# Loads behind the table, limits over three engines, late full stores and a staggered first unit in an attention and feed-forward kernel

## The chip, the core and the metric

One Trainium2 chip, of which the kernel uses one core. The metric is the time of one execution in device microseconds (us). Five engines run their own instruction streams and meet at semaphores: TensorE (PE; its weight loads are listed as PEld), VectorE (DVE), ScalarE (ACT), GpSimd (POOL) and SyncE (SP), which here only issues DMAs.

## The reference

Attention with a learned relative bias for 4 batches, 8 heads, 576 positions and head size 64, then a feed-forward part with a cosine gate over the 2304 rows.

```
scores = q @ k.T / sqrt(64)
x      = log1p(|i-j|) / log1p(max(i,1))         # per row i and column j
bias   = relu(x * w1 + b1) @ w2                 # 32 hidden values -> 8 heads
scores = scores + bias                          # the same for all batches
attn   = softmax(scores);  out = attn @ v       # [4, 8, 576, 64]
x      = out as [2304, 512]
h      = x @ w_in                               # 512 -> 2048
result = (h * cos(h)) @ w_out                   # 2048 -> 512
```

All in float32. The kernel gets two small tables besides: `ltab` = log1p of 0..575, and `pack` with 1/log1p(max(i,1)), w1, b1 and w2 laid out by partition.

## The kernel before

There are three stages: the bias rows, the attention units, the feed-forward part.

**Bias rows (to about 51 us).** The bias depends on the positions and the head alone. Since relu(x*w1+b1) scales, the kernel takes `wl = ltab*w1` (one value per hidden unit and distance) and `edge` = log1p(i)*b1 and computes for each query i a hidden row `ht = max(wl + edge[i], 0)`. Sixteen queries make a group: four `ht` tiles of 128 partitions (four queries of 32 hidden units each), three or four of them on VectorE (line 341) and the rest on ScalarE (line 339); TensorE multiplies by the negated w2 (line 356); ScalarE scales with `mrow` and writes `rt` (line 374), and SP stores the 128 rows of 591 values to a scratch tensor `sc` in DRAM (line 375). There are 36 groups, in the order of bias tiles 4, 0, 1, 2, 3. A bias tile `bt` (128 queries x 576 keys of one head) is then read back from `sc` with a skewed pattern (`load_bias`, lines 273 and 286). Line 397 says after which group which bias tile is loaded.

At the start ScalarE's queue issues the load of `lt` (`ltab` to all partitions), SP that of `pk` (`pack`), and both go on with k and q of the first two units. VectorE prepares `edge` in four quarters of 32 partitions and a corner (lines 326 and 327), ScalarE `wl` (line 328).

**Units (51 to about 290 us).** A unit is a pair of heads hp and a batch b, 16 in all, hp outermost; each has five tiles of queries in the order 0, 1, 4, 2, 3. One (unit, tile) is a job and gets a slot; `slot(i)` (line 616) writes the order of the work by hand: the scores of job i (`qk`, line 431), exp of job i-1 on ScalarE (line 471), its scaling by 1/sum on GpSimd (line 494), the turning of job i-3's probabilities on TensorE (`halves`, line 501) with copies to SBUF on ScalarE and VectorE, the product with v (line 569), and the split of q and k of later units in high and low parts on GpSimd (lines 186, 190). `qk` writes two score tiles `s`, one per head, of which there are two buffers in all; each head takes six matmuls with 64 rows (two halves of the keys, three products of high and low parts), and the heads alternate. VectorE adds the bias and takes the row minimum of the negated scores (line 453) and with that frees the buffer.

`load_w` brings a weight in float32, `abs_w` (line 92, ScalarE) is the first to read it, in slot 9, and line 100 (VectorE) goes on. Line 724 issues the first two weights in slots 5 and 6.

**Feed-forward (to the end).** Matmuls with w_in (line 759) and w_out (line 805) take turns on TensorE.

All DMAs but those of ScalarE's queue are issued by SP in program order. Eight semaphores are used in turn for the DMAs, so that an issue waits until the DMA eight before it has landed.

Of the kernel before, what the change touches and what calls it, by code (L numbers as in the profile page):

```python
# [9 lines left out]
F32 = mybir.dt.float32  # L10
# [3 lines left out]
AF = mybir.ActivationFunctionType  # L14
ALU = mybir.AluOpType
# [13 lines left out]
def kernel(  # L29
# [11 lines left out]
    nc = tc.nc  # L41
    B, H, S, D = q.shape
# [4 lines left out]
    NQ = S // 16  # L47
    RB = S + 15
    PITCH = S + 32
    GP = 16 * (8 * PITCH - 1)  # L50
    HALF = S // 2
# [14 lines left out]
    xT = const.tile([128, HP, NT], F32, name="xT")  # L66
    xs = const.tile([128, 2, KD, TB], F32R, name="xs")
    wpre = [const.tile([128, 2, 2, 512], F32R, name=f"wpre{i}") for i in range(WPRE)]
    sc = [dram.tile([1, (8 if t < 4 else 4) * GP + 16], F32, name=f"sc{t}") for t in range(5)]
# [7 lines left out]
    def load_w(fc, part):  # L77
        r = wk.tile([128, 512, 2], U32, tag="raw", name="raw")
        if part == 0:
            nc.sync.dma_start(  # L80
                out=r.rearrange("p (c x) y -> p c (x y)", c=KD),
                in_=w_in[:, fc * 256 : fc * 256 + 256].rearrange("(c p) x -> p c x", p=128),
            )
        else:
            nc.sync.dma_start(out=r.rearrange("p x y -> p (x y)"), in_=w_out[fc * 128 : fc * 128 + 128, :])
        raw[fc, part] = r
# [25 lines left out]
    with tc.manual_schedule():  # L112
# [14 lines left out]
        lt = ca.tile([128, S], F32, name="lt")  # L127
# [5 lines left out]
        qTs = [st.tile([128, 2, 640], F32R, name=f"qT{i}") for i in range(2)]  # L133
# [19 lines left out]
        def load(u, x, pieces=None, queue=None):  # L153
            hp, b = units[u]
            src = {"q": q, "k": k, "v": v}[x]
            pair_ = src[b, 2 * hp : 2 * hp + 2]
            if x == "v":
                t = vN[u % 2]
                for h in range(2):
                    nc.sync.dma_start(  # L160
                        out=t[:, 4 * h : 4 * h + 4, :], in_=pair_[h, 0:512].rearrange("(c p) d -> p c d", p=128)
                    )
                for h in range(2):
                    nc.sync.dma_start(out=t[64 * h : 64 * h + 64, 8 + h, :], in_=pair_[h, 512:576])
                return
            if (u, x) not in nat:
                m = 5 if x == "k" else 4
                nat[u, x] = (lk if x == "k" else ld).tile([128, m, 2, D], F32, tag=x, name=f"n{x}")
            t = nat[u, x]
            todo_ = [(t[:, 0:4, h], pair_[h, 0:512].rearrange("(p r) d -> p r d", r=4)) for h in range(2)]  # L170
            if x == "k":
                for i, o in ((q, 0), (k, 64)):
                    todo_.append((t[o : o + 64, 4], i[b, 2 * hp : 2 * hp + 2, 512:576].rearrange("h p d -> p h d")))
            for o, i in todo_ if pieces is None else [todo_[n] for n in pieces]:
                (queue or nc.sync).dma_start(out=o, in_=i)
# [16 lines left out]
        kN = {}  # L192
# [104 lines left out]
        ra = opened(stage, "ra", 8, "left")  # L297
# [3 lines left out]
        wl = ca.tile([128, S], F32, name="wl")  # L301
        pk = ca.tile([128, pack.shape[1]], F32, name="pk")
        edge = ca.tile([128, S // 4], F32, name="edge")
        nbd = ca.tile([128, 32], F32, name="nbd")
        nc.sync.dma_start(out=pk[:, 0:178], in_=pack[:, 0:178])
        load(0, "k")
        load(0, "q", queue=nc.scalar)
        for x in "kq":
            load(1, x)
        wparts = [(fc, p) for fc in range(WPRE) for p in range(2)]  # L310
        mi, w1c, b1c = pk[:, 0:144], pk[:, 144:145], pk[:, 145:146]
        bd = pk[:, 146:178]
# [7 lines left out]
        for s in range(4):  # L320
            nc.tensor.matmul(
                pm[32 * s : 32 * s + 32, 0:NQ], pick, mi[:, s : 4 * NQ : 4], start=True, stop=True, tile_position=(0, 32 * s)
            )
        for g in range(4):
            r = slice(32 * g, 32 * g + 32)
            nc.vector.tensor_scalar(edge[r], lt[r, g:S:4], b1c[r], None, ALU.mult)
        nc.vector.tensor_scalar(edge[0:32, 0:1], lt[0:32, 1:2], b1c[0:32], None, ALU.mult)
        nc.scalar.activation(out=wl, in_=lt, func=AF.Copy, scale=w1c)

        def bias_hid(k):  # L330
            qi = groups[todo[k][0]][todo[k][1]]
# [13 lines left out]
        def bias_rows(k, hts):  # L345
# [17 lines left out]
                    )  # L363
            return ps[:, at : at + RB]

        def bias_store(k, ps):
            t, gi = todo[k]
            qi = groups[t][gi]
            rt = ra.tile([128, RB], F32, tag="r", name="rt")
            m = mrow[:, qi : qi + 1]  # L370
            if k == len(todo) - 2:
                nc.vector.tensor_scalar(rt, ps, m, None, ALU.mult)
            else:
                nc.scalar.activation(out=rt, in_=ps, func=AF.Copy, scale=m)
            nc.sync.dma_start(
                out=bass.AP(sc[t].tensor, sc[t].offset + gi * GP, [[PITCH, 128], [1, RB]]),
                in_=rt,
            )

        tiles = [0, 1, 4, 2, 3]  # L380
        for i in range(WPRE):
# [4 lines left out]
        SECOND = {6: ("k", (0,)), 7: ("k", (1,)), 8: ("k", (2,)), 9: ("k", (3,)), 10: ("q", (0,)), 11: ("q", (1,))}  # L386
        todo = [(t, gi) for t in (4, 0, 1, 2, 3) for gi in range(len(groups[t]))]
        held, hts = None, bias_hid(0)
        nc.vector.tensor_copy(mrow, pm[:, 0:NQ])
        for n in range(len(todo) + 1):  # L390
            now = hts
            if n < len(todo):
                hts = bias_hid(n + 1) if n + 1 < len(todo) else None
                ps = bias_rows(n, now)
            if held:
                bias_store(*held)
            for t, heads in {13: ((4, ()),), 20: ((0, (0,)),), 21: ((0, (1,)),), 28: ((1, (0,)),), 29: ((1, (1,)),)}.get(n, ()):
                load_bias(0, t, heads)
            if n == len(todo):
                load_bias(0, 2)  # L400
                load(3, "k", (2, 3))
                load_bias(0, 3)
            held = (n, ps)
            if n in SECOND:
                load(2, *SECOND[n])
            if n in T_FIRST:
                halved[n] = turn(*T_FIRST[n], bank())
                keep_hi(*T_FIRST[n], halved[n])
            if n - 1 in T_FIRST:
                keep_lo(*T_FIRST[n - 1], halved[n - 1])  # L410
# [16 lines left out]
            PX[u, hf] = px.tile([128, WQ[hf]], F32, tag=f"x{hf}", name=f"PX{hf}")  # L427

        cur = {}

        def qk(u, j):
            t = tiles[j]
            heads = range(2 if t < 4 else 1)
            s = [ps_s.tile([128, 2, 512], F32, tag="s", name="s") for h in heads]
            for hf in range(2):
                for n, (a, b) in enumerate(((0, 0), (0, 1), (1, 0))):
                    for h in heads:
                        r = slice(64 * h, 64 * h + 64) if t < 4 else slice(0, 128)
                        o = HALF * hf + (64 if h == 0 else 0)
                        nc.tensor.matmul(  # L440
                            s[h][:, hf, 0:HALF],
                            qTs[u % 2][r, a, 128 * t : 128 * t + 128] if t < 4 else qTs[u % 2][:, a, 512:640],
                            kN[u][r, b, o : o + HALF],
                            start=(n == 0),
                            stop=(n == 2),
                            tile_position=(r.start, 0),
                        )
            hp = units[u][0]
            P[u, j] = pp.tile([128, 1152], F32, tag="p", name="P")
            for h in heads:  # L450
                neg = P[u, j][:, 576 * h : 576 * h + 576]
                m = sv.tile([128, 2], F32, tag=f"m{h}", name="m")
                nc.vector.tensor_tensor_reduce(  # L453
                    neg.rearrange("p (a x) -> p a x", a=2),
                    s[h][:, :, 0:HALF],
                    bias[hp, t, h].rearrange("p (a x) -> p a x", a=2),
                    1.0,
                    3.0e38,
                    ALU.add,
                    ALU.min,  # L460
                    m[:, 0:1],
                )
                cur[u, j, h] = (neg, m)
# [131 lines left out]
        W_MID = [(3, 9)]  # L595
        W_PLAN = [(0, 2), (0.5, 3), (1, 7), (2, 8), ("load", 8), (4, 12)]
        W_LATE = 10
        REST = {2: (1, 2), 3: (3, 4)}
        get = lambda i: jobs[i] if 0 <= i < len(jobs) else None

# [15 lines left out]
        def slot(i):  # L616
# [101 lines left out]
            if now:  # L718
                if i == 1:
                    load(0, "v")  # L720
                for du, x in LOAD_PLAN[j]:
                    if u + du < NU:
                        load(u + du, x, (0, 1) if (u, x) == (0, "k") else None)
                if i in (5, 6):
                    load_w(*wparts[i - 5])
                hp, b = units[u]
                if b == B - 1 and hp + 1 < HP:
                    load_bias(hp + 1, tiles[j])
                if i in X_EARLY:
                    split_x(0, 0, X_EARLY.index(i))  # L730
# [228 lines left out]
```

## Time and profile before

| | |
|---|---|
| median of 3 runs | 695.43 us (694.91 to 697.91) |
| the profiled execution | 695.13 us, its span 693.3 us |
| TensorE busy | 679.7 us (98%) |
| VectorE, ScalarE, GpSimd busy | 580.8 (84%), 435.8 (63%), 398.2 us (57%) |
| DMA | 58.57 MB, 84 GB/s on average; 345 to 351 GB/s from 30 to 50 us |
| granted clock of TensorE | 1.0 throughout |

The shares are averages over stages with different limits: in the bias rows VectorE, ScalarE and TensorE are all nearly full; in the first unit none is, and from there on TensorE is. Busy time counts no DMA issues.

### The profile page before, as it was taken

What the parts mean: (1) busy time and instruction counts of PE and PEld (TensorE: products, weight loads), DVE (VectorE), ACT (ScalarE), POOL (GpSimd) and SP (SyncE); (2) the same over time, 40 slices, a digit from 0 to 9 for tenths busy, and PEclk for the clock granted to TensorE, in tenths of its full rate; (3) what the DMA queues carried; (4) which work ended last, traced back from release to release, by engine and by line L of the source; (5) the groups of instructions that cost most, each with busy time, mean ns of one, the idle gap of its engine ahead of it and who ended that gap; (6) DMA issues with size and microseconds to landing.
All of it is one profiled execution on the core that took longest, in us unless ns stands there. A gap on an engine that the chain in (4) does not pass through costs nothing.

```text
span 693.3 us, 15601 instructions
## 1 busy us (share of the span) xinstructions
PE 679.7 (98%) x5747; PEld 561.9 (81%) x5747; DVE 580.8 (84%) x1345; ACT 435.8 (63%) x938; POOL 398.2 (57%) x480
## 2 busy tenths in 40 slices
PE   6998999999999999999999999999999999999997
PEld 3666777777777777799989898998988888999986
DVE  8998888888888888678788789999899899876666
ACT  6998888988889887545565554454544544433342
POOL 0008888898988989646456356265374474463300
PEclk9999999999999999999999999999999999999999
DMA  6798546437337311012011111110111110011112
GB/s 161 266 350 224 130 122 168 104 85 220 71 92 200 99 50 41 10 31 61 30 34 60 30 49 44 32 61 32 34 58 31 57 35 32 0 46 46 47 46 92
DMA packets 84445, 58.57 MB, mean 84 GB/s; under 512 B 62224, under 2 KB 70800, under 8 KB 84368
## 3 DMA queue, kind: packets, MB, share of 16 engines
q1 hardware_dynamic: 83024, 56.88, 28.4%
q8 instruction: 46, 0.75, 0.5%
q10 hardware_dynamic: 1344, 0.69, 0.4%
q14 instruction: 31, 0.25, 0.1%
HBM read 41.94 MB, written 15.61 MB: 83 GB/s over the span
## 4 chain that ended last, share of the span: by engine, by line
PE 93%; DMA 3%; DVE 1%; POOL 1%; ACT 1%; issue 0%; SPq 0%; DVEq 0%; POOLq 0%
PE ph L759 29%; PE po L805 29%; PE pv L569 12%; PE s L440 11%; PE pm L501 6%; PE pa L356 4%; DMA sc<-rt 2%; PE pt L501 1%; PE spare L501 1%; DMA lt<-in_ltab_dram 1%; DMA bt<-sc 1%; POOL P L494 0%; DVE ht L341 0%; ACT ht L339 0%; DVE acc L829 0%
## 5 line engine op out<-in xcount | busy, mean ns | idle before, releaser
L453 DVE CUSTOM_DVE_ANT_0 P<-s,bt 128x576 f32<-128x576 f32 x144 | 103.8, 753 | 24.4 <-PE s L440 24.1
L494 POOL TENSOR_SCALAR P<-P,rc 128x576 f32<-128x576 f32 x144 | 108.3, 764 | 24.3 <-DVE rc L487 11.5
L763 ACT ACTIVATE a<-ph,quarter 128x384 int32<-128x384 f32 x96 | 55.7, 581 | 97.8 <-PE ph L759 96.9
L555 POOL TENSOR_TENSOR xs<-xT,xs 128x384 fp32r<-128x384 f32 x96 | 108.1, 1126 | 8.0
L471 ACT ACTIVATE P<-P,m 128x576 f32<-128x576 f32 x144 | 110.0, 768 | 0.6 <-DVE m L453 0.6
L759 PE MATMUL ph<-xs,wpre 128*128 128x384 f32 x576 | 109.4, 338 | 0.0
L759 PE MATMUL ph<-xs,w 128*128 128x384 f32 x576 | 108.5, 337 | 0.0
L774 ACT ACTIVATE r<-r,hpi 128x384 f32<-128x384 f32 x96 | 59.3, 617 | 74.8 <-DVE r L770 74.6
L759 PEld LDWEIGHTS ph<-xs,wpre 128*128 128x128 f32 x576 | 101.9, 188 | 5.4 <-DVE a L778 0.9
L759 PEld LDWEIGHTS ph<-xs,w 128*128 128x128 f32 x576 | 101.3, 188 | 5.1 <-DVE a L778 1.2
L769 DVE SCALAR_TENSOR_TENSOR r<-a,ph 128x384 f32<-128x384 int32 x96 | 52.8, 550 | 62.7 <-ACT a L763 62.6
L440 PE MATMUL s<-kN,qT 64*128 64x288 f32 (+1 forms) x864 | 92.0, 311 | 2.0 <-DVE m L453 1.4
L440 PEld LDWEIGHTS s<-kN,qT 64*128 64x128 f32 (+1 forms) x864 | 70.7, 185 | 27.2 <-DVE dn L484 7.6
L554 POOL TENSOR_SCALAR xs<-xT 128x384 fp32r<-128x384 f32 x96 | 63.2, 658 | 29.7 <-PE ph L759 29.7
L788 DVE TENSOR_TENSOR gl<-a,gh 128x384 fp32r<-128x384 f32 x96 | 75.8, 789 | 0.4 <-ACT gh L782 0.4
L569 PE MATMUL pv<-PT,vN 128*64 128x320 f32 (+1 forms) x512 | 76.0, 418 | 0.0
L805 PE MATMUL po<-wpre,gh 128*128 128x512 f32 x288 | 75.3, 397 | 0.0
L805 PE MATMUL po<-w,gh 128*128 128x512 f32 x288 | 75.2, 395 | 0.0
L110 POOL TENSOR_TENSOR w<-wb,w 128x512 fp32r<-128x512 f32 x16 | 20.8, 1297 | 87.6 <-ACT w L108 87.6
L782 ACT ACTIVATE gh<-a 128x384 fp32r<-128x384 f32 x96 | 49.8, 518 | 23.6 <-DVE a L778 23.6
L770 DVE SCALAR_TENSOR_TENSOR r<-a,r 128x384 f32<-128x384 int32 x96 | 61.0, 636 | 3.3
L805 PEld LDWEIGHTS po<-wpre,gh 128*128 128x128 f32 x288 | 53.4, 188 | 9.4 <-issue 0.5
(98 smaller groups left out, 1166.8 us busy)
## 6 DMA issues: line engine op xcount, KB each, us to landing
sc<-rt SPq DMA_DIRECT2D x36, 295.5 KB, 4.5
raw<-in_moe_w_in_dram SPq DMA_DIRECT2D x16, 512.0 KB, 3.7
raw<-in_moe_w_out_dram SPq DMA_DIRECT2D x16, 512.0 KB, 3.5
bt<-sc SPq DMA_DIRECT2D x16, 288.0 KB, 4.0
out_dram<-acc SPq DMA_DIRECT2D x17, 256.0 KB, 2.0
nk<-in_k_dram SPq DMA_DIRECT2D x32, 128.0 KB, 3.5
bt<-sc SPq DMA_DIRECT2D x16, 256.0 KB, 4.2
vN<-in_v_dram SPq DMA_DIRECT2D x32, 128.0 KB, 2.8
```

The source lines that it names most:

```text
L440: nc.tensor.matmul(s[h][:, hf, 0:HALF], qTs[u % 2][r, a, 128 * t : 128 * t + 128] if t < 4 else qTs[u % 2][:, a, 512:640], kN[u][r, b, o : ...
L453: nc.vector.tensor_tensor_reduce(neg.rearrange("p (a x) -> p a x", a=2), s[h][:, :, 0:HALF], bias[hp, t, h].rearrange("p (a x) -> p a x", ...
L471: nc.scalar.activation(out=P[u, j][:, 576 * h : 576 * h + 576], in_=neg, func=AF.Exp, bias=m[:, 0:1], scale=-1.0, accum_out=dn[u, j][:, h ...
L494: nc.gpsimd.tensor_scalar(p, p, r, 1.0, ALU.mult, ALU.mult)
L554: nc.gpsimd.tensor_scalar(h, src, 1.0, 1.0, ALU.mult, ALU.mult)
L555: nc.gpsimd.tensor_tensor(l, src, f(h), ALU.subtract)
L569: nc.tensor.matmul(ps[64 * h : 64 * h + 64, 0 : WQ[hf]], a, m, start=(c == 0), stop=(c == 4), tile_position=(0, 64 * h), skip_group_check= ...
L759: nc.tensor.matmul(ps, a, x, start=(i == 0), stop=(i == 3 * KD - 1))
L770: nc.vector.scalar_tensor_tensor(r, n, -TWO_PI_LO, r, ALU.mult, ALU.add)
L774: nc.scalar.activation(out=r, in_=r, func=AF.Sin, scale=SIN_SCALE, bias=hpi)
L788: nc.vector.tensor_tensor(gl, a, f(G[key][0]), ALU.subtract)
L805: nc.tensor.matmul(O[n][i], a[:, 128 * i : 128 * i + 128], w, start=(i0 == 0 and p == 0), stop=(i0 == GF - 1 and p == 2),)
```

## The change

Three parts. (1) At the start: SP waits for `lt` before it issues any load of k or q (`keepalive_nop` with `lt` as its input), and also issues the q of the first unit, which ScalarE's queue did. `wl` is made by VectorE; the quarters of `edge` by VectorE (two), ScalarE and GpSimd; the corner of `edge` and `mrow` by ScalarE, behind its first `ht`. (2) The last eleven groups of rows are written into the not yet used part of `xT` and not into the pool `ra`. At once only the rows of the first pair of heads are stored (two DMAs of 16 rows each); the full store of all 128 rows follows in slots 6 to 14. The loads of bias tile 2 move up to groups 33 and 34, and the first two weights are issued in slots 8 and 9. (3) In the first unit the second head's six matmuls lag three behind the first head's.

```diff
         nc.sync.dma_start(out=pk[:, 0:178], in_=pack[:, 0:178])
-        load(0, "k")
-        load(0, "q", queue=nc.scalar)
-        for x in "kq":
-            load(1, x)
+        nc.sync.keepalive_nop(ins=[nc.sync.lower_ap(lt)])
+        for u in range(2):
+            for x in "kq":
+                load(u, x)
...
+        nc.vector.tensor_scalar(wl, lt, w1c, None, ALU.mult)
         for g in range(4):
             r = slice(32 * g, 32 * g + 32)
-            nc.vector.tensor_scalar(edge[r], lt[r, g:S:4], b1c[r], None, ALU.mult)
-        nc.vector.tensor_scalar(edge[0:32, 0:1], lt[0:32, 1:2], b1c[0:32], None, ALU.mult)
-        nc.scalar.activation(out=wl, in_=lt, func=AF.Copy, scale=w1c)
+            if g == 3:
+                nc.gpsimd.tensor_scalar(edge[r], lt[r, g:S:4], b1c[r], 1.0, ALU.mult, ALU.mult)
+            elif g == 2:
+                nc.scalar.activation(out=edge[r], in_=lt[r, g:S:4], func=AF.Copy, scale=b1c[r])
+            else:
+                nc.vector.tensor_scalar(edge[r], lt[r, g:S:4], b1c[r], None, ALU.mult)
...
+        rest = xT[:, 1:].rearrange("p h n -> p (h n)")
+        late = [rest[:, RB * i : RB * i + RB] for i in range(11)]
+
+        def store_rows(k, rt):
+            t, gi = todo[k]
+            nc.sync.dma_start(
+                out=bass.AP(sc[t].tensor, sc[t].offset + gi * GP, [[PITCH, 128], [1, RB]]),
+                in_=rt,
+            )
+
         def bias_store(k, ps):
             t, gi = todo[k]
             qi = groups[t][gi]
-            rt = ra.tile([128, RB], F32, tag="r", name="rt")
+            n = k - len(todo) + len(late)
+            rt = late[n] if n >= 0 else ra.tile([128, RB], F32, tag="r", name="rt")
...
+            if n < 0:
+                store_rows(k, rt)
+            else:
+                for h in range(2):
+                    nc.sync.dma_start(
+                        out=bass.AP(sc[t].tensor, sc[t].offset + gi * GP + h * PITCH, [[8 * PITCH, 16], [1, RB]]),
+                        in_=rt[h:128:8],
+                    )
...
-        nc.vector.tensor_copy(mrow, pm[:, 0:NQ])
+        nc.scalar.activation(out=edge[0:32, 0:1], in_=lt[0:32, 1:2], func=AF.Copy, scale=b1c[0:32])
+        nc.scalar.activation(out=mrow, in_=pm[:, 0:NQ], func=AF.Copy)
...
+        STAGGERED = (0,)
...
+            lag = 3 if u in STAGGERED and t < 4 else 0
+            for x in range(6 + lag):
+                for h in heads:
+                    if not 0 <= x - lag * h < 6:
+                        continue
+                    hf, n = divmod(x - lag * h, 3)
...
+        STORES = {6: (0, 1), 7: (2, 3), 10: (4, 5), 11: (6, 7), 12: (8,), 13: (9,), 14: (10,)}
...
-                if i in (5, 6):
-                    load_w(*wparts[i - 5])
+                if i in (8, 9):
+                    load_w(*wparts[i - 8])
+                for n in STORES.get(i, ()):
+                    store_rows(len(todo) - len(late) + n, late[n])
```

What stands on SP at the start before, with what each issue waits for (`nk` and `nq` are k and q as they lie in DRAM; DMAHW0 is the semaphore of `lt`, DMAHW1 that of `pk`):

```order
L305 DMA pk<-in_pack_dram 128x178
L175 DMA nk<-in_k_dram 128x4x64 x2
L175 DMA nk<-in_q_dram 64x2x64
L175 DMA nk<-in_k_dram 64x2x64
L175 DMA nk<-in_k_dram 128x4x64
L175 DMA nk<-in_k_dram 128x4x64 [waits DMAHW1_49]
L175 DMA nk<-in_q_dram 64x2x64 [waits DMAHW2_49]
```

And now:

```order
L305 DMA pk<-in_pack_dram 128x178
L175 DMA nk<-in_k_dram 128x4x64 [waits DMAHW0_49]
L175 DMA nk<-in_k_dram 128x4x64
L175 DMA nk<-in_q_dram 64x2x64
L175 DMA nk<-in_k_dram 64x2x64
L175 DMA nq<-in_q_dram 128x4x64 x2
L175 DMA nk<-in_k_dram 128x4x64 [waits DMAHW0_49]
```

Before, the first five loads wait for nothing; now the first waits for `lt`, and all behind it on SP with it. The two loads of `nq` have come over from ScalarE's queue.

VectorE from its last set-up copy to the first hidden rows, before:

```order
L315 COPY pick<-ident 128x32
L318 TENSOR_SCALAR nbd<-pk 128x32
L326 TENSOR_SCALAR edge<-lt,pk 32x144 x4
L327 TENSOR_SCALAR edge<-lt,pk 32x1
L341 TENSOR_SCALAR ht<-wl,edge 128x528 x3
L389 COPY mrow<-pt 128x36
L341 TENSOR_SCALAR ht<-wl,edge 128x544 x3
```

And now:

```order
L315 COPY pick<-ident 128x32
L318 TENSOR_SCALAR nbd<-pk 128x32
L324 TENSOR_SCALAR wl<-lt,pk 128x576
L332 TENSOR_SCALAR edge<-lt,pk 32x144 x2
L345 TENSOR_SCALAR ht<-wl,edge 128x528 x3
L345 TENSOR_SCALAR ht<-wl,edge 128x544 x3
```

Two quarters of `edge`, the corner and `mrow` have left VectorE, and `wl` has come. The first `ht` now waits for ScalarE and GpSimd too, which make the other quarters.

TensorE in slot 1 of the first unit, before (the number of `s` tells the head's tile; the first of twelve matmuls that alternate so):

```order
L440 MATMUL s_1051<-kN_303,qT0_107 128x288
L440 MATMUL s_1052<-kN_303,qT0_107 128x288
L440 MATMUL s_1051<-kN_303,qT0_107 128x288
L440 MATMUL s_1052<-kN_303,qT0_107 128x288
L440 MATMUL s_1051<-kN_303,qT0_107 128x288
L440 MATMUL s_1052<-kN_303,qT0_107 128x288
```

And now, all twelve:

```order
L464 MATMUL s_1052<-kN_304,qT0_107 128x288 x4
L464 MATMUL s_1053<-kN_304,qT0_107 128x288
L464 MATMUL s_1052<-kN_304,qT0_107 128x288
L464 MATMUL s_1053<-kN_304,qT0_107 128x288
L464 MATMUL s_1052<-kN_304,qT0_107 128x288
L464 MATMUL s_1053<-kN_304,qT0_107 128x288 x4
```

The first head's last matmul is the ninth and not the eleventh, three of the second head's stand alone at the end, and three (with the start of the fourth) of the first head's alone at the beginning.

## Rows read from the trace of the kernel before

**Rows 1.** Busy time by stretch (length, then us busy, instructions, clock, DMA share, GB/s).

```profile
52.00:64.00 12.00, 9.27 (x109) 7.27 (x109) 9.43 (x33) 9.83 (x26) 9.51 (x14) 1.00 0.83 241
54.00:72.00 18.00, 15.45 (x211) 12.08 (x211) 14.87 (x53) 15.53 (x42) 17.37 (x24) 1.00 0.83 224
64.00:274.00 210.00, 210.00 (x2835) 156.32 (x2833) 182.72 (x618) 179.21 (x469) 187.00 (x244) 1.00 0.46 117
```

**Rows 2.** The chain of waits, its beginning (start, length, what).

```profile
0.73 4.04 DMA lt<-in_ltab_dram
```

**Rows 3.** Timeline of VectorE in the bias rows (start, length, idle time before it).

```profile
4.80 1.42 DVE L326 TENSOR_SCALAR edge<-lt,pk 32x144 f32<-32x144 f32 x4 [0.15 <-DMA lt<-in_ltab_dram]
...
6.38 1.28 DVE L341 TENSOR_SCALAR ht<-wl,edge 128x528 f32<-128x528 f32 x3
7.59 0.17 DVE L389 COPY mrow<-pt 128x36 f32<-128x36 f32 x1
7.70 8.30 DVE L341 TENSOR_SCALAR ht<-wl,edge 128x544 f32<-128x544 f32 x19
...
22.82 27.06 DVE L341 TENSOR_SCALAR ht<-wl,edge 128x464 f32<-128x464 f32 x80
```

**Rows 4.** Timeline of ScalarE at the third hidden row.

```profile
9.82 0.76 ACT L339 ACTIVATE ht<-wl,edge 128x560 f32<-128x560 f32 x1 [2.13 <-PE pa L356]
```

**Rows 5.** DMA issues (KB each, median us to landing), 10-15 us, then 600 us on.

```profile
sc<-rt SPq DMA_DIRECT2D x3, 295.5 KB, 3.2
...
out_dram<-acc SPq DMA_DIRECT2D x17, 256.0 KB, 2.0
```

**Rows 6.** Timeline of VectorE, the reductions of slots 3 and 4.

```profile
59.38 0.76 DVE L453 CUSTOM_DVE_ANT_0 P<-s,bt 128x576 f32<-128x576 f32 x1 [0.32 <-PE s L440]
...
61.87 0.76 DVE L453 CUSTOM_DVE_ANT_0 P<-s,bt 128x576 f32<-128x576 f32 x1 [0.31 <-PE s L440]
...
62.92 0.76 DVE L453 CUSTOM_DVE_ANT_0 P<-s,bt 128x576 f32<-128x576 f32 x1 [0.29 <-DMA bt<-sc]
```

**Rows 7.** Timeline of TensorE, scores in slots 0 and 2, turning in slot 8.

```profile
51.05 1.05 PE L440 MATMUL s<-kN,qT 64*128 64x288 f32 x12
...
56.21 1.06 PE L440 MATMUL s<-kN,qT 128*128 128x288 f32 x6
...
72.51 0.78 PE L501 MATMUL pm<-ident,P 64*128 64x64 f32 x16
```

**Rows 8.** Timeline of GpSimd, its first work in the units, and slots 6 and 7.

```profile
53.98 0.73 POOL L186 TENSOR_SCALAR kN<-kt 128x640 fp32r<-128x640 f32 x1 [52.67 <-DVE kt L248]
...
71.06 3.08 POOL L494 TENSOR_SCALAR P<-P,rc 128x576 f32<-128x576 f32 x4
```

**Rows 9.** Lines 100 and 492: shortest, median, longest ns.

```profile
L100 DVE TENSOR_SCALAR wb<-wb x32: 406/730/1230, 86.7 to 594.2; 128x512 f32<-128x512 f32 x32
...
L492 POOL TENSOR_SCALAR P<-P,rc x16: 309/313/328, 62.0 to 275.3; 128x64 f32<-128x64 f32 x16
```

**Rows 10.** Timeline of SP, issues around the first weight.

```profile
57.82 1.50 SPq L273 DMA_DIRECT2D bt<-sc  x3
...
66.67 0.59 SPq L80 DMA_DIRECT2D raw<-in_moe_w_in_dram  x1
...
67.90 1.25 SPq L175 DMA_DIRECT2D nk<-in_k_dram  x2
```

**Rows 11.** The first two weights' transfers, to 100 us.

```profile
DMA to landing us min/median/max: 4.1/5.3/6.5
```

**Rows 12.** Timeline of ScalarE, its last row and slot 9.

```profile
51.21 0.76 ACT L374 ACTIVATE rt<-pa,mrow 128x591 f32<-128x591 f32 x1 [1.08 <-issue]
...
75.61 0.66 ACT L92 ACTIVATE wb<-raw 128x512 f32<-128x512 f32 x1
76.83 0.60 ACT L529 ACTIVATE PT<-pm 128x512 f32<-128x512 f32 x1 [0.56 <-PE pm L501]
78.09 0.44 ACT L529 ACTIVATE xT<-pv 128x320 f32<-128x320 f32 x1 [0.67 <-PE pv L569]
```

More of the change, by code (lines that the diff above doesn't have):

```diff
@@ L374, in bias_store @@
                 nc.scalar.activation(out=rt, in_=ps, func=AF.Copy, scale=m)
[L375 to L378, printed above, removed]
+            if n < 0:
[6 more added lines that the diff above has]
+                    )
         tiles = [0, 1, 4, 2, 3]
@@ L396 @@
                 bias_store(*held)
-            for t, heads in {13: ((4, ()),), 20: ((0, (0,)),), 21: ((0, (1,)),), 28: ((1, (0,)),), 29: ((1, (1,)),)}.get(n, ()):
+            for t, heads in {13: ((4, ()),), 20: ((0, (0,)),), 21: ((0, (1,)),), 28: ((1, (0,)),), 29: ((1, (1,)),), 33: ((2, (0,)),), 34: ((2, (1,)),)}.get(n, ()):
                 load_bias(0, t, heads)
             if n == len(todo):
-                load_bias(0, 2)
                 load(3, "k", (2, 3))
@@ L434, in qk @@
             s = [ps_s.tile([128, 2, 512], F32, tag="s", name="s") for h in heads]
[L435 to L447, printed above, removed]
+            lag = 3 if u in STAGGERED and t < 4 else 0
[4 more added lines that the diff above has]
+                    hf, n = divmod(x - lag * h, 3)
+                    a, b = ((0, 0), (0, 1), (1, 0))[n]
+                    r = slice(64 * h, 64 * h + 64) if t < 4 else slice(0, 128)
+                    o = HALF * hf + (64 if h == 0 else 0)
+                    nc.tensor.matmul(
+                        s[h][:, hf, 0:HALF],
+                        qTs[u % 2][r, a, 128 * t : 128 * t + 128] if t < 4 else qTs[u % 2][:, a, 512:640],
+                        kN[u][r, b, o : o + HALF],
+                        start=(n == 0),
+                        stop=(n == 2),
+                        tile_position=(r.start, 0),
+                    )
             hp = units[u][0]
```

## The prediction

> **What bounds the kernel now.** I read the busy times by stretch first, then the chain of waits, then the timelines of the engines at the places that the change touches. From 64 to 274 us TensorE is busy for all of 210.00 us [rows 1], and so it stays to the end: whatever reaches TensorE earlier at 64 us brings the end nearer by the same amount, and nothing after 64 us is worth anything while its cover lasts. The front is where time can be won, and it has two halves.
>
> In the first half, the bias rows, the pace is VectorE's. It does its last 80 `ht` between 22.82 and 49.88 us, 0.338 us apart, with no gap in them [rows 3], and the first rows begin when VectorE is done with its preparations: the table `lt` takes 4.04 us from 0.73 us [rows 2], VectorE starts on it at 4.80 and on the first `ht` at 6.38 [rows 3]. So time won ahead of 6.38 goes through to the end of the rows one for one, as long as ScalarE and TensorE keep up.
>
> In the second half, the first unit (52 to 64 us), TensorE is busy 9.27 of 12 us and so idle for 2.73; VectorE has 9.43 and ScalarE 9.83 [rows 1]. GpSimd is the fullest: 17.37 of 18 us from 54 to 72 [rows 1]. The chain of waits runs through row stores and a bias tile's load here, and the bias tile of the fifth slot is indeed waited for at 62.92. But that wait is 0.29 us [rows 6]. The transfers thus stand beside other work almost to their full length, and taking 2.4 MB of stores out of them (11 groups, 295.5 KB less a quarter each) is worth 0.29 us by itself.
>
> **The change part by part.** All against the profiled run's own 695.13 us, of which 693.3 are the span and 1.8 lie around it and stay. The median of the runs is 695.43, so 0.3 us above.
>
> 1. *Loads behind the table.* Today eight loads of k and q are on their way with `lt`. In the change SP issues only `pk`, then waits for `lt`. What `lt` (288 KB) then takes, no row shows. Lower bound of the gain: 0 us, if the 4.04 us are its own; below nothing is excluded, since nothing is put ahead of it. Upper bound: stores of 256 KB that run alone take 2.0 us [rows 5], so 4.04 - 2.0 = 2.04 us. The row nearest in size and setting is a store of 295.5 KB in the light stretch from 10 to 15 us: 3.2 us [rows 5]. I take it: the gain is 4.04 - 3.2 = **0.84 us**. The loads of k and q start later for it by nearly as much as the table takes; four groups of rows, at over three times 0.338 us of VectorE each, stand ahead of the first turning that reads them, and cover it.
>
> 2. *VectorE's preparations.* Removed: four `edge` from 4.80 and a small fifth, 1.58 us until the first `ht`; and the copy `mrow`, which moves the next `ht` from 7.59 to 7.70 [rows 3]. Added: `wl`, of the form and size of an `ht`, which stand 8.30/19 = 0.437 us apart [rows 3]; kept: two `edge` at 1.42/4 = 0.355. That is 0.44 + 0.71 = 1.15, and 0.05 for the handing over: 1.20. Gain 1.58 - 1.20 = 0.38 us, and 0.11 for `mrow`: **0.49 us**. The other two quarters of `edge` run on ScalarE and GpSimd beside it. GpSimd's price is not shown; its scaling of 128x64 takes 313 ns and of 128x576 about 1.48/2 = 0.74 [rows 8, 9], so 144 columns lie between, some 0.4 us by the line through both, far inside 1.15. ScalarE gets a quarter, the corner of `edge` and `mrow` and loses `wl`; it stands idle for 2.13 us ahead of 9.82 [rows 4], which covers them.
>
> 3. *Second head three matmuls behind.* In the pairs of today, two half-height matmuls run side by side: twelve of them take 1.05 us, and six of full height 1.06 [rows 7]. Per step that is about 0.15 us, so a lone half costs as much as a pair. The staggered form has nine steps for six: 3 x 0.15 = 0.45 us of TensorE more for each of four tiles, 1.8 in all, against 2.73 us of idle. For it the first head's matmuls run while VectorE still reads the second head's old scores. What that can win is what VectorE waits for scores in slots 3 and 4: 0.32 + 0.31, and with the bias tile's 0.29 it is 0.92 us [rows 6]. Yet I take **0 us**, for GpSimd stands in the way: from 53.98 us it works without a gap that matters, and its scaling of the sixth tile, the first two of the four instructions from 71.06, is done at 71.06 + 3.08/2 = 72.6, while TensorE starts to turn that tile at 72.51 [rows 7, 8]. TensorE's second half of that turning could come 0.2 us sooner, no more, unless GpSimd itself starts sooner. GpSimd starts once k of the next unit is copied, behind turnings on TensorE that the first staggered tile holds up by 0.45 us, of which most is covered by VectorE's two reductions ahead of the copy. So: between -0.2 and +0.2. What is late next, when the scores are not, is the scaled tile.
>
> 4. *Eleven groups stored in two parts.* Early parts: 22 issues in place of 11, and a quarter of the bytes. Their gain is the 0.29 us above, inside the same cap: 0 us. The full stores go out in slots 6 to 14; 11 x 295.5 KB are 3.25 MB on queues whose share is 0.46 there [rows 1], and the next hp's bias loads come only in slot 15. Cost 0 while two things hold: SP runs ahead of the slots, and the first weight is there when ScalarE wants it. That second one is a rival below.
>
> Sum: 0.84 + 0.49 + 0 + 0 = 1.33 us, and 695.13 - 1.33 = **693.8 us**.
>
> By the Trainium skill, "DMA: Bandwidth & Descriptors", section on the anatomy of one DMA, a transfer costs about 2.0 us and its bytes at 436 GB/s (measured there on another path); an estimate from it for `lt` is 2.7 us, the gain 1.35 and the sum 693.3. The row of 3.2 us is dearer than its rule, and I stay with the row.
>
> **The rivals.**
>
> *The table lands no sooner.* Then the part that gives the change its name does nothing. For it: nothing excludes it, as no row shows the table by itself. Against: 2.0 and 3.2 us for transfers of its size elsewhere [rows 5]. 695.13 - 0.49 = 694.6.
>
> *GpSimd and VectorE get in each other's way.* Both start when `lt` lands, on the same tile. For it: L100, a scaling on VectorE from and to the same memory, takes 406 ns at best and 1230 at worst in the stretches where GpSimd works [rows 9]: up to 0.82 us of being held. Against: GpSimd's piece is small, and may come second. If held for GpSimd's 0.4 us, VectorE's preparations end at 1.60 and not 1.20, as late as today: 693.8 + 0.4 = 694.2, at worst 694.6. The Trainium skill, "SBUF — State Buffer", section on the two separate sides, states such a rule: VectorE in its two-port modes and GpSimd share a port pair, whoever starts first has it for the whole instruction and the other stands. L100's spread agrees with it; who comes first here, no run shows.
>
> *The stagger pays in full.* If GpSimd can be earlier too (its copies come sooner), the 0.92 us arrive: 693.8 - 0.92 = 692.9. Against: its gapless row.
>
> *The lone halves are paid in TensorE's time* and the kernel is slower than before. Place: slots 0 to 4. If the waits of TensorE there are not where the lone steps fall, 1.8 us come on top: 693.8 + 1.8 = 695.6. It decides once TensorE has less than 1.8 us of idle left at these places; 2.73 speaks against it.
>
> *The weight comes late.* Today SP issues the first weight at 66.67, 8.85 us behind the bias tile's load at 57.82; ten more issues now stand ahead of it (four late stores, six loads), at up to 1.25/2 = 0.63 each: 15.2 us [rows 10]. The bias load itself can go at about 54.4 (ScalarE's last row ends at 51.97 [rows 12], less 1.33; then two issues, at no more than 0.63 for both, and 3.2 to land), so the weight leaves at 69.6 and lands 4.1 to 6.5 us later [rows 11], at 73.7 to 76.1. ScalarE wants it at 75.61 - 1.33 = 74.3 [rows 12]. It then stands for up to 1.8 us, of which its own waits of 0.56 and 0.67 [rows 12] cover 1.2: 0 to 0.6 us, so at worst 694.4.
>
> **How the numbers follow.** The forecast, 693.8 us, has 0.54; its own range, from 0.6 us more out of the table's load to 0.6 less with the stagger's 0.2, is 693.0 to 694.6. The table no sooner 0.15, the port 0.12, the stagger in full 0.08, the lone halves 0.06, the weight 0.05. The range of 8 in 10 takes in the best table (693.8 - 1.2 = 692.6) with part of the stagger below, and the lone halves above: **692.2 to 695.8**. About 0.5% (3.5 us) is what a measurement of this kernel can tell from no change; from 695.43 that is below 691.9 or above 698.9. Below lies only the full stagger with the best table: 691.7, with what I overlook 0.09. Above lies none of the cases; the lone halves, a late weight and a table no sooner together give 697.0. For what isn't listed 0.04. The rest, 0.87, is within.
>
> **What would show it.** Right: `lt` lands near 3.9 us after the start and the first `ht` begins near 5.2; the 80 `ht` are still gapless; no wait for `bt` in slot 4; TensorE full from about 62.4; GpSimd gapless from 52.6. Step 3 is wrong if GpSimd's scaling of the sixth tile ends earlier, measured from the first score matmul, than now. The weight rival shows as a wait of ScalarE for `raw` in slot 9. The prediction falls if the first `ht` gains less than 0.7 us, or if the gain at the first `ht` is not found again at the end.

## The result and the profile after

The change made the kernel slower: 702.81 us median (700.45 to 703.29 in 5 runs) against 695.66, a ratio of 1.0094 (95% interval 1.0079 to 1.0108). 693.8 was predicted. The profiled execution took 700.45 us, the fastest of the five, with a span of 698.7; before, 695.13 and 693.3.

Where the time went can be read from two marks on TensorE: the first scores (slot 0) and the scores of slot 11. Before they start at 51.05 and 80.46 us, and 612.8 us are left to the end. After (timeline of TensorE; start, length, idle time before it):

```profile
50.31 1.17 PE L464 MATMUL s<-kN,qT 64*128 64x288 f32 x12
...
60.73 1.08 PE L464 MATMUL s<-kN,qT 64*128 64x288 f32 x5 [1.10 <-DVE m L477]
...
65.81 0.60 PE L464 MATMUL s<-kN,qT 64*128 64x288 f32 x1 [2.42 <-DVE m L477]
67.66 1.80 PE L464 MATMUL s<-kN,qT 64*128 64x288 f32 x11 [1.25 <-DVE m L477]
...
85.80 1.14 PE L464 MATMUL s<-kN,qT 64*128 64x288 f32 x12
```

And before, in slots 5 and 11:

```profile
63.75 1.05 PE L440 MATMUL s<-kN,qT 64*128 64x288 f32 x11 [0.66 <-DVE m L453]
...
80.46 1.15 PE L440 MATMUL s<-kN,qT 64*128 64x288 f32 x12
```

The rest is 698.7 - 85.80 = 612.9 us, as before. The first scores come 0.74 us sooner; from there to slot 11 it takes 35.49 us where it took 29.41. So 6.1 us are lost in the first slots, and the rows above say in slots 4 and 5: 4.8 us of waits, and behind them eleven matmuls in 1.80 us that took 1.05 before. What TensorE waits for is VectorE's minimum, and VectorE waits for bias tiles (its timeline, to be compared with [rows 6]):

```profile
59.91 0.76 DVE L477 CUSTOM_DVE_ANT_0 P<-s,bt 128x576 f32<-128x576 f32 x1 [1.13 <-DMA bt<-sc]
64.99 0.76 DVE L477 CUSTOM_DVE_ANT_0 P<-s,bt 128x576 f32<-128x576 f32 x1 [3.58 <-DMA bt<-sc]
66.84 0.76 DVE L477 CUSTOM_DVE_ANT_0 P<-s,bt 128x576 f32<-128x576 f32 x1 [1.09 <-DMA bt<-sc]
```

That is 5.8 us of waiting for bias tiles where it was 0.29. Were the queues slow? No: from 50 to 56 us they are busy for a share of 0.40 at 102 GB/s (before, 1.04 at 373).

```profile
50.00:56.00 6.00, 5.59 (x58) 4.74 (x57) 3.68 (x13) 4.58 (x11) 2.58 (x4) 1.00 0.40 102
```

The tiles were asked for late. SP's timeline:

```profile
42.26 3.76 SPq L394 DMA_DIRECT2D sc<-xT  x6
46.07 0.93 SPq L273 DMA_DIRECT2D bt<-sc  x1
47.10 1.10 SPq L394 DMA_DIRECT2D sc<-xT  x2
48.24 1.05 SPq L273 DMA_DIRECT2D bt<-sc  x2
49.40 4.91 SPq L394 DMA_DIRECT2D sc<-xT  x8
54.35 0.58 SPq L273 DMA_DIRECT2D bt<-sc  x1
55.03 1.10 SPq L394 DMA_DIRECT2D sc<-xT  x2
56.17 1.05 SPq L273 DMA_DIRECT2D bt<-sc  x2
57.33 2.98 SPq L394 DMA_DIRECT2D sc<-xT  x4
...
61.94 1.40 SPq L273 DMA_DIRECT2D bt<-sc  x3
```

From 42.26 us on SP issues almost without a gap, and it issues the last early part at 59.72 us, though ScalarE was done with those rows at 51.2. The 22 early parts take a median of 0.587 us of SP each, 12.8 us in all; a whole store took a median of 0.437 before, and the last eleven 5.9 in all, waits included. By line, before and after (shortest, median, longest ns):

```profile
L375 SPq DMA_DIRECT2D sc<-rt x14: 319/437/1370, 38.9 to 52.0; - x14
```

```profile
L394 SPq DMA_DIRECT2D sc<-xT x22: 472/587/1084, 42.3 to 59.7; - x22
```

The early parts do not wait for landings: the DMA eight before was issued 4.9 us earlier, and a part lands in 2.4. The last tile's loads leave at 61.94; the kernel before had its at 57.82 [rows 10]. The chain of waits after agrees:

```profile
59.72 0.59 SPq L394
...
62.91 3.77 DMA bt<-sc
...
66.84 0.76 DVE P L477
```

Behind the first of these waits TensorE's clock fell, too. Busy time by stretch (PE, PE's weight loads, VectorE, ScalarE, GpSimd; then the granted clock, DMA share, GB/s), after:

```profile
60.00:61.00 1.00, 0.27 (x2) 0.27 (x4) 1.00 (x4) 0.62 (x3) 1.00 (x2) 0.86 0.19 52
...
66.00:67.00 1.00, 0.41 (x1) 0.09 (x1) 0.16 (x1) 0.65 (x2) 0.00 (x0) 0.50 0.64 149
...
69.00:70.00 1.00, 1.00 (x16) 1.00 (x15) 0.73 (x3) 0.00 (x0) 1.00 (x2) 0.50 0.70 158
...
71.00:72.00 1.00, 1.00 (x12) 0.55 (x10) 0.85 (x6) 1.00 (x4) 0.56 (x1) 1.00 0.48 141
```

For 10 us it stands at 0.50, 1.2 GHz and not 2.4; before it was 1.00 there [rows 1].

The start, after (VectorE's timeline, then GpSimd's), where [rows 3] had the first `ht` at 6.38:

```profile
4.30 0.52 DVE L324 TENSOR_SCALAR wl<-lt,pk 128x576 f32<-128x576 f32 x1
4.74 0.95 DVE L332 TENSOR_SCALAR edge<-lt,pk 32x144 f32<-32x144 f32 x2
5.83 9.43 DVE L345 TENSOR_SCALAR ht<-wl,edge 128x528 f32<-128x528 f32 x22
```

```profile
4.44 0.76 POOL L328 TENSOR_SCALAR edge<-lt,pk 32x144 f32<-32x144 f32 x1 [3.14 <-DMA lt<-in_ltab_dram]
```

The first `ht` gains 0.55 us, not 1.22.

### The profile page after: what moved, and what is told of

The parts are those of the page before. It is cut to its first block, busy times and chain, and to the rows that moved or that the text cites. A ratio compares the mean times of both kernels' runs of the same rounds, so it can differ in the third digit from the quotient of the medians.

```text
span 698.7 us, 15616 instructions
## 1 busy us (share of the span) xinstructions
PE 682.4 (98%) x5747; PEld 565.0 (81%) x5747; DVE 581.2 (83%) x1342; ACT 435.8 (62%) x940; POOL 397.4 (57%) x481
## 4 chain that ended last, share of the span: by engine, by line
PE 94%; DVE 2%; ACT 1%; DMA 1%; issue 1%; SPq 0%; DVEq 0%; ACTq 0%
PE ph L786 29%; PE po L832 29%; PE pv L593 12%; PE s L464 11%; PE pm L525 6%; PE pa L360 5%; PE pt L525 1%; PE spare L525 1%; DVE P L477 1%; DMA bt<-sc 1%; DMA pk<-in_pack_dram 0%; DVE ht L345 0%; ACT ht L343 0%; DVE acc L856 0%; ACT rt L389 0%
## 5 line engine op out<-in xcount | busy, mean ns | idle before, releaser
L464 PE MATMUL s<-kN,qT 64*128 64x288 f32 (+1 forms) x864 | 94.6, 315 | 5.2 <-DVE m L477 4.8
L464 PEld LDWEIGHTS s<-kN,qT 64*128 64x128 f32 (+1 forms) x864 | 73.3, 188 | 30.1 <-DVE dn L508 8.1
```

The lines of the kernel that those rows point to most:

```text
L464: nc.tensor.matmul(s[h][:, hf, 0:HALF], qTs[u % 2][r, a, 128 * t : 128 * t + 128] if t < 4 else qTs[u % 2][:, a, 512:640], kN[u][r, b, o : ...
```

## The experiments

My theory (A): SP's time for each issue, whatever its size, made the bias tiles late. Rivals: the small 16-row transfers are slow themselves (B); the second head's lag (C) or the start (D) costs the time. Then: what the low clock adds (K), what the lag is worth, and who holds up whom at the start. All results first. The two marks are those from above and, like the waits, of the one profiled execution; from slot 11 to the end every profile has 612.7 to 613.2 us.

| run | median us | ratio to before (95%) | first scores | to slot 11 | VectorE's waits for bt |
|---|---|---|---|---|---|
| before | 695.66 | | 51.05 | 29.41 | 0.3 |
| changed kernel | 702.81 | 1.0094 (1.0079-1.0108) | 50.31 | 35.49 | 5.8 |
| 1 whole at once | 697.3 | 1.0030 (1.0017-1.0043) | 51.56 | 32.74 | 2.2 |
| 2 whole in two DMAs | 703.1 | 1.0109 (1.0094-1.0124) | 50.32 | 37.87 | 7.2 |
| 3 split, two queues | 695.33 | 1.0000 (0.9991-1.0008) | 51.55 | 29.60 | 0 |
| 4 start only | 695.17 | 0.9992 (0.9983-1.0000) | 51.10 | 29.21 | 0 |
| 5 filler | 701.44 | 1.0090 (1.0074-1.0105) | 50.30 | 34.95 | 5.2 |
| 6 long filler | 700.99 | 1.0077 (1.0057-1.0096) | 51.38 | 34.62 | 5.4 |
| 7 two queues, no lag | 695.35 | 0.9995 (0.9986-1.0003) | 51.40 | 29.38 | 0 |
| 8 lag only | 695.5 | 0.9993 (0.9982-1.0004) | 51.80 | 29.12 | 0 |
| 9 start without GpSimd | 694.6 | 0.9987 (0.9975-0.9999) | 50.84 | 29.18 | 0 |
| 10 eleven tiny DMAs | 699.02 | 1.0046 (1.0032-1.0060) | 51.57 | 32.78 | 1.6 |
| 11 two queues, new start | 695.22 | 0.9994 (0.9979-1.0009) | 51.08 | 31.88 | 0.9 |
| 12 split the last five | 698.66 | 1.0043 (1.0026-1.0060) | 51.03 | 32.78 | 3.1 |

**1, 2: one issue or two, the same bytes.** Both are the changed kernel without the later stores. Run 1, then run 2 (`...` stands for code that is left out, here and below):

```diff
-                for h in range(2):
-                    nc.sync.dma_start(
...
-                        in_=rt[h:128:8],
-                    )
+                store_rows(k, rt)
```

```diff
                 for h in range(2):
                     nc.sync.dma_start(
...
-                        in_=rt[h:128:8],
+                        in_=rt[64 * h : 64 * h + 64],
                     )
```

> The changed kernel, but each of the last eleven groups goes out whole and at once in one DMA; no later stores. The start and the lag of the second head stay. Theory A (SP's time for each issue, 0.55 to 0.63 us whatever the size, is what made the bias tiles late): 11 issues fewer take 11 x 0.55 = 6 us off SP between 42 and 62 us, the tiles wait for no bias again, TensorE's clock stays at 1.0, and what is left is the start's gain of 0.74 us: 694.7 us. Theory B (the transfers of 16 rows are slow in the queues, not in their issue): none of them is left, so 694.7 as well; this run does not tell A from B. Theory C (the lag's lone half-height matmuls cost it): the lag is still there, so 700 to 703.

> As the run before, whole rows at once and no later stores, but each of the eleven groups in two DMAs of 64 rows: the same bytes at the same place, the issues doubled, and no DMA of 16 rows. Theory A (the count of issues on SP): SP is as full as in the changed kernel, its issues in this stretch again near 0.55 to 0.6 us each, the bias tiles of the third and fourth tile late by 3 us and more, TensorE's clock at half for some us: 700 to 703 us. Theory B (the 16-row shape): nothing is late, 694.7. Theory C (the lag): 700 to 703, but without waits for bias tiles.

The two differ in nothing but the count of issues, and by 5.8 us. SP in run 2:

```profile
49.85 4.94 SPq L394 DMA_DIRECT2D sc<-xT  x8
...
57.86 3.28 SPq L394 DMA_DIRECT2D sc<-xT  x4
...
63.53 1.27 SPq L273 DMA_DIRECT2D bt<-sc  x3
```

That is 0.62 us an issue for 64 rows, and 0.61 for 16 in the changed kernel: between these two, bytes make no difference. B and C fall: run 2 has no 16-row DMA and is as slow, and the lag is in both runs. Run 1 missed its 694.7, though. Its executions lie between 695.26 and 700.14 us, and the profiled one, of 699.0, is among the slow ones. In it three loads of bias tile 2, from 50.93 to 53.35 us, stand ahead of the last stores, and with whole stores, 5.5 us to land, SP also waits for the landing of the eighth DMA before (2.3 us in six waits). The last store left at 54.33 (before: 52.02) and landed 5.33 us later, and the bias tiles of slot 4 were waited for:

```profile
53.57 1.08 SPq L375 DMA_DIRECT2D sc<-xT  x2
...
59.73 1.28 SPq L273 DMA_DIRECT2D bt<-sc  x3
```

```profile
62.79 0.76 DVE L473 CUSTOM_DVE_ANT_0 P<-s,bt 128x576 f32<-128x576 f32 x1 [1.35 <-DMA bt<-sc]
...
64.45 0.76 DVE L473 CUSTOM_DVE_ANT_0 P<-s,bt 128x576 f32<-128x576 f32 x1 [0.90 <-DMA bt<-sc]
```

So moving up the loads of tile 2 seems to cost something when the stores stay whole; no run has that move alone, so this is not shown.

**3: the same 22 parts, half of them on GpSimd's queue.**

```diff
-                    nc.sync.dma_start(
+                    (nc.gpsimd if h else nc.sync).dma_start(
```

> The changed kernel with its early parts as they are, 22 DMAs of 16 rows, and the later stores; only the second head's part is issued from GpSimd's queue, which has no DMA of its own then. Theory A: SP's issues in the stretch fall back to their old number, the bias tiles are on time, 694.7 us, or up to 1 us more if GpSimd's issues hold up its own first work near 52 us. Theory B (slow 16-row transfers): as many of them as before, the tiles late, 700 to 703. Theory C (the lag): 700 to 703 without waits for bias tiles.

The loss is gone with every 16-row transfer, the lag and the later stores still there. SP's last early parts and the last tile's loads:

```profile
52.86 1.11 SPq L394 DMA_DIRECT2D sc<-xT  x2
...
57.05 2.20 SPq L273 DMA_DIRECT2D bt<-sc  x3
```

This, with the pair before, is what shows A. The 1.2 us that its scores of slot 6 win (13.98 us after the first scores; before, 15.19) are lost again by slot 11.

**4, 9: the start alone, with and without GpSimd.** Both are the kernel before with the change's first part; in 9 ScalarE makes two quarters of `edge` (the diff is against run 4).

```diff
-            if g == 3:
-                nc.gpsimd.tensor_scalar(edge[r], ...)
-            elif g == 2:
+            if g >= 2:
                 nc.scalar.activation(out=edge[r], ...)
```

> The kernel before with the first part of the change alone: the loads of k and q behind the table, and wl, edge and mrow shared out over three engines. Theory A: the first ht near 5.83 us as in the changed kernel, the score matmuls 0.7 us sooner, no bias tile late, 694.7 us. Theory D (the start's loads, late by 4 us, or ScalarE's extra pieces, come back as a wait later in the front): the first ht sooner, but the first scores no sooner than 51.05 us, 695.4 or more.

> The kernel before with the first part of the change, but the quarter of edge that GpSimd scales goes to ScalarE, which then has two. Theory P (GpSimd and VectorE get in each other's way at the start): VectorE's two quarters go back from 0.95 us to 0.71, ScalarE's two take 1.1, and the first ht starts some 0.3 us sooner after the table than with GpSimd, 694.9 us. Theory Q (VectorE's quarters are slower for another reason, and no port is shared): the two still take 0.95, the first ht starts as late after the table as with GpSimd, 695.2.

VectorE in run 4, then in run 9:

```profile
4.84 0.95 DVE L332 TENSOR_SCALAR edge<-lt,pk 32x144 f32<-32x144 f32 x2
5.93 1.30 DVE L345 TENSOR_SCALAR ht<-wl,edge 128x528 f32<-128x528 f32 x3
```

```profile
4.83 0.68 DVE L330 TENSOR_SCALAR edge<-lt,pk 32x144 f32<-32x144 f32 x2
5.62 1.71 DVE L343 TENSOR_SCALAR ht<-wl,edge 128x528 f32<-128x528 f32 x4
```

With `lt` at the same time, VectorE's quarters take 0.68 us in place of 0.95 and the first `ht` starts 0.3 us sooner: theory P. The Trainium skill, "SBUF — State Buffer", on the two separate sides, has VectorE in its two-port modes and GpSimd take turns at a port pair for a whole instruction; the trace agrees, with 0.27 us. Run 9 is the only version that beats the kernel before, by 0.13% (0.01 to 0.25%). As a cause of the 7 us D falls. Its sign, first scores no sooner than 51.05, was met in run 4 (51.10), but that profile has a wait of VectorE for TensorE in the first rows (0.62 us) that the profile before has not (last section). Two profiles with the old start and such a wait, of runs 8 and 10, have their first scores at 51.80 and 51.57.

**7, 8: the lag.** Run 7 is run 3 with `STAGGERED = ()`, run 8 the kernel before with the lag.

> The run with the second head's early part on GpSimd's queue, without the lag of the second head's scores. The prediction's step 3 (the lag is worth nothing, GpSimd's gapless row stands in the way): 695.3 us as with it. The lag pays: 0.6 to 0.9 us more, 696.1. The lag costs (lone half-height matmuls): 694.5 or less.

> The kernel before with the lag alone. Step 3 of the prediction: 695.6 us, within 0.2 us of before, and GpSimd's scaling of the sixth tile as late after the first scores as before. The rivals on record: in full 0.92 us less, 694.7; or the lone halves paid in TensorE's time, 1.8 us more, 697.4.

Taking it out or putting it in changes nothing that the intervals tell. GpSimd's scaling of the sixth tile starts at 71.72 us in run 8:

```profile
71.72 2.94 POOL L499 TENSOR_SCALAR P<-P,rc 128x576 f32<-128x576 f32 x4
```

That is 19.92 us after the first scores; before it was 71.06 - 51.05 = 20.01 [rows 7, 8]. GpSimd gives 0.1 us. Runs 3 and 7 say the same, with 19.90 and 20.00.

**5, 6: TensorE kept busy in its waits.** Matmuls whose results nobody reads, 6, 13 and 6 of them in run 5, 24 for the 13 in run 6.

```diff
+        FILL = {(0, 4, 3, 1): 6, (1, 0, 0, 0): 13, (1, 0, 0, 1): 6}
...
+                    for _ in range(FILL.get((u, j, x, h), 0)):
+                        nc.tensor.matmul(fill[:, 0:HALF], qTs[0][:, 0, 512:640], kN[0][:, 0, 0:HALF], ...)
```

> The changed kernel, with matmuls put into TensorE's waits that compute nothing that is used: 6 of 128x288 ahead of the second head's scores of the fifth tile, 13 ahead of the sixth tile's scores and 6 behind their first matmul (1.06 us for six in the kernel before), so that TensorE is busy while the bias tiles are late. SP and the bias tiles are as in the changed kernel. Three theories of what the low clock adds. K1, it adds what is done at half rate after the last wait: 11 matmuls in 1.80 us for 1.05, and the turnings and products up to 71.6 us, about 1.5 us in all: 701.2 us. K2, the low clock is most of the loss: 699 or less. K3, it is only a companion of the wait and costs nothing: 702.8. In all three the bias tiles land as late as before.

> The filler run with 24 in place of 13 matmuls ahead of the sixth tile's scores, since 13 (1.97 us) ended 1.65 us before the scores could go on, and TensorE's clock then fell from 67.4 to 70.5 us. Theory K1 (the low clock adds only what is done at half rate after the last wait, some 1.5 us): the granted clock stays at 1.0, the scores' other 11 matmuls take 1.05 us and not 1.63, 700.5 to 701.2. K2 (the clock is most of the loss): 699 or less. K3 (it costs nothing): 702.8.

In run 5 the filler ended 1.65 us before the scores could go on, and the clock fell later instead (0.50 from 68 to 70 us): inconclusive. In run 6 it stayed up:

```profile
60.00:72.00 12.00, 11.49 (x116) 9.80 (x116) 6.23 (x22) 6.64 (x18) 7.68 (x12) 1.00 0.65 157
```

```profile
68.35 1.05 PE L472 MATMUL s<-kN,qT 64*128 64x288 f32 x11 [0.51 <-DVE m L485]
```

The eleven matmuls behind the last wait took 1.05 us. VectorE's waits stayed at 5.4 us and the way to slot 11 at 34.62. So the clock has 35.49 - 34.62 = 0.9 us of the 6.1 by the profiles and 1.8 by the medians, whose intervals overlap; the wait itself has the rest. K2 falls. K1 fits both; by the medians alone K3 is not excluded.

**10: eleven tiny DMAs in the kernel before.** `junk` is a tensor in DRAM that nobody reads.

```diff
+            if k >= len(todo) - 11:
+                nc.sync.dma_start(out=junk[len(todo) - 1 - k : len(todo) - k, 0:64], in_=rt[0:1, 0:64])
```

> The kernel before, with one more DMA behind each of its last eleven stores, on SP too: 256 bytes of the same rows to a place in DRAM that nobody reads. It adds next to no bytes and no wait for anyone but SP's time to issue it. Theory A (the count of issues on SP): 11 x 0.55 to 0.63 = 6.1 to 6.9 us of SP between 42 and 60 us, of which SP's own waits take up one or two; the bias tiles of the third and fourth tile late by some us, TensorE's clock at half for a time, 700 to 702 us. Theory B (the queues are slow with small rows): the tiny DMAs move nothing, 695.6. If the rows' buffers are held for longer and ScalarE waits for them, that is a cost of this run's own and would show as a wait on rt.

2.8 KB in all cost 3.4 us: count, not bytes. But it is less than A says, and for the most part not by A's way. SP's waits from 42 to 60 us (total, times, longest):

```profile
SPq L382 <- DMA sc<-rt: 1.7, 3, 1.0
SPq L377 <- DMA sc<-rt: 1.3, 3, 0.5
```

An issue here waits until the DMA eight before it has landed, and each tiny one takes one of the eight turns from stores that take 4 us to land. The loads of bias tile 2 leave at 56.05 us, 3.6 later than before, and SP's standstills for landings ahead of them are 3.2 us longer. A tiny one's own issue took only 0.29 us, also where it followed another issue at once, as seven of the eleven did. So a DMA more costs a turn where transfers are long, and SP's time for its issue where they are short; run 10 did not show the second by itself.

**11, 12: repairs.** 11 joins runs 3 and 9; 12 splits only the last five groups.

> The changed kernel with two repairs: the second head's early part on GpSimd's queue, and GpSimd's quarter of edge on ScalarE. If the two repairs add up: 0.3 us ahead of the run with two queues, 694.8 to 695.0; if the front is paced by GpSimd alone from 54 us (gapless there), its start, 0.3 us sooner, sets it: 695.0. If the bias tiles, now on time, had been worth 0.3 us as well: 694.3.

> The changed kernel with only its last five groups stored in two parts, the six ahead of them whole and at once: 16 issues in place of 22. Theory A: SP is 6 x 0.57 = 3.4 us ahead of the changed kernel at the last tile's loads, the waits for bias tiles fall from 5.8 us to some 2.5, 698 to 699 us. If the bytes bound it as much as the issues (1.3 MB more than in the changed kernel): no better than whole at once, 697.3. If the fault were the lag or the start: 702.8.

Run 12 came out as A said, 698.66 us with waits of 3.1, though its last tile's loads leave at 59.87 us, 2.1 ahead of the changed kernel and not 3.4. Run 11 can't be told from run 3: its interval holds both no gain and the 0.3 us hoped for. Its profile is of an execution of 697.93 us, its slowest, with a wait of 0.90 us for a bias tile and the clock down behind it (last section); the other eleven lie between 694.76 and 696.06.

## Why the prediction was wrong

**The step that failed** is the fourth: "22 issues in place of 11, and a quarter of the bytes", at "cost 0 while ... SP runs ahead of the slots". I priced the bytes and not the issues. The price stood in a row: 1.25 us for two loads, 0.63 each [rows 10]. For the early parts I wrote "two issues, at no more than 0.63 for both", on which the bias load was to leave at 54.4; two took 1.2, and it left at 61.94. Set against the rows' pace the sum is plain: the last eleven groups are done between 40.9 and 51.2 us, 1.03 us apart, and two issues are 1.2 us; with the bias loads between them SP is 8.5 us behind at the last one. Nor does a smaller DMA issue faster: a part took 0.587 us where a whole store took 0.437, so the early parts held SP for 12.8 us where the eleven whole stores held it for 5.9. Runs 2 and 3 show that this is the cause. No rival had it: SP appears in the weight rival only, for a later transfer. (ScalarE did wait for the weight, 1.33 us in slot 9; from slot 11 to the end nothing is lost.)

**Steps 1 and 2** had the right sign and were too large. `lt` landed at 4.28 us and not 4.77: 0.49 gained, 0.84 taken. (Seven loads, not eight, had been on their way with it: the second `nq` was issued at 4.79.) The preparations took 5.83 - 4.30 = 1.53 us, where 1.58 went to 1.20 in the forecast; the 0.11 for `mrow` came (the fourth `ht` starts at 7.05 and not 7.70). That is the port rival: GpSimd's quarter took 0.76 us, not 0.4, and VectorE's two 0.95, not 0.71. That rival said 1.60 and "as late as today". The prediction's own condition, a gain of less than 0.7 us at the first `ht`, was met with 0.55. By run 4 the whole start is worth 0.4 us at the end (0 to 1.2 by its interval). The prediction let a gain there go through one for one "as long as ScalarE and TensorE keep up"; in ten of the fourteen profiles VectorE waits for TensorE in the first rows.

**Step 3** was right: 0 us, and GpSimd's scaling of the sixth tile starts only 0.1 us sooner, within the 0.2 that it allowed (runs 3, 7 and 8; run 3 loses at slot 11 what it won at slot 6, where TensorE then waits 0.8 us for ScalarE's copies and 0.4 for GpSimd). Lone halves cost nothing either: in run 8 the way to slot 11 is 0.3 us shorter, not 1.8 longer.

**The sum.** From the forecast 693.8 to the profiled 700.45: 0.6 us less from the start (0.74 for 1.33), 6.1 us lost between slots 0 and 11, of which 0.9 to 1.8 are the clock. The median execution is 2.4 us longer than the profiled one, and no trace shows where. With SP relieved (run 3) the change is worth nothing, where 1.33 us had been forecast.

## What to carry to other kernels

Price a transfer that is split twice: its bytes on the queues and its issues on the engine that issues them, and set the issues of one round against the round's length. A queue that is half empty says nothing on whether its issuer is. Where a late load makes TensorE wait, expect the clock to add to it, but look for the load first.

## What the runs showed of the hardware

An issue on SP took 0.32 us where SP had stood waiting (run 1, whole stores). Right behind one another, parts of 16 rows took 0.587 us (changed kernel), parts of 64 rows 0.594 (run 2), whole stores of 128 rows 0.41 (before); a whole store right behind a tiny DMA took 0.32 (run 10). So it does not go by the bytes, and more rows can cost less. What sets it is not shown.

The granted clock fell behind small waits in run 11. TensorE waited 0.26 and 0.49 us there, and stood at 0.50 from 64 to 69 us, though busy for all of it:

```profile
62.10 0.40 PE L523 MATMUL pm<-ident,P 64*128 64x64 f32 x6 [0.26 <-POOL P L516]
...
63.37 1.80 PE L462 MATMUL s<-kN,qT 64*128 64x288 f32 x11 [0.49 <-DVE m L475]
```

```profile
64.00:69.00 5.00, 5.00 (x41) 3.74 (x41) 2.69 (x12) 3.54 (x12) 4.89 (x7) 0.50 0.86 240
```

In the kernel before waits of 0.28 us in slot 4 and 0.66 in slot 5 left it at 1.00. What decides is not shown.

TensorE's first matmuls are slow for a time that differs between executions. The 512-column matmuls of the rows from 10.4 to 10.8 us (busy, mean ns), in the changed kernel and in run 1:

```profile
L360 PE MATMUL pa<-ht,nbd 128*32 128x512 f32 x6 | 1.1, 600 | 0.0
```

```profile
L360 PE MATMUL pa<-ht,nbd 128*32 128x512 f32 x6 | 1.9, 1061 | 0.0
```

The rows of the granted clock say 1.00 for this time, but the trace's first record of the clock starts at 9.53 us in the changed kernel, 12.50 in run 1 and 10.46 before; ahead of it 1.00 means only that no record stands there. In all fourteen profiles the last of these matmuls to take over 900 ns starts 0.6 to 1.3 us ahead of that record, so the slow phase may be the low clock; no record shows it. In run 1 VectorE then waits 0.68 and 0.25 us for TensorE, and its first scores come at 51.56 though its first `ht` began at 6.01. Ten of the fourteen profiles have such a wait, of 0.5 to 0.7 us; those of the kernel before and of the changed kernel have none. That is why a gain at the start is read from medians here and not from one profile.

A DMA issue on GpSimd's queue can be held while VectorE is busy. In run 3 seven issues took 6.80 us:

```profile
46.53 6.80 POOL L394 DMA_DIRECT2D sc<-xT  x7 [0.68 <-ACT xT L389]
```

The first of the seven alone took 3.95 us, to 50.47, when VectorE's last `ht` had ended (50.38); the six behind it took 0.48 each. Run 7 has one of 3.95 us to 50.33 (last `ht` to 50.23), run 11 one of 6.10 us to 50.01 (49.91). Why that one issue and not those ahead of it, at 0.52 to 0.89 us, is not shown.
